# Sorted k^T copied into block order, and first FFN pieces by pairs of heads, in a block-sorted attention kernel with a squared-ReLU FFN

## The chip, the cores and the metric

The kernel runs on one core of a Trainium2 chip. The metric is the device time of one execution in microseconds; each figure is the median of several executions. The spread of the kernel before over its first three runs was 223.69 to 226.38 us. The profile is of one execution; its span (first to last instruction) is 1.5 to 2 us shorter than the device time. PE is TensorE, PEld its weight load, DVE VectorE, ACT ScalarE, POOL GpSimd, SP the engine that issues most DMAs here, and SPq its sequencer. A run counts as slow when it lies over 1.5% above the fastest of its kernel; verdicts use the fast runs alone. The clock quoted is the one granted to TensorE, 1.000 being full speed.

## The reference, cut to what matters

```python
# q, k, v: 4 batches x 8 heads x 768 x 64; sort_net: 4 x 8 x 8 x 8
P = sort_net
for _ in range(5):                      # Sinkhorn: softmax over rows, then columns
    ...
k_sorted = einsum('bhij,bhjcd->bhicd', P, k_blocks)   # blocks of 96 rows
v_sorted = einsum('bhij,bhjcd->bhicd', P, v_blocks)
scores = q_blocks @ k_sorted_blocks.T / sqrt(64)      # within a block only
attn = softmax(scores) @ v_sorted_blocks
x = attn as (3072 tokens, 512)
h = maximum(x @ w_in, 0)                # w_in 512 x 2048
out = (h * h) @ w_out                   # w_out 2048 x 512
```

The work is done in bf16 with sums in float32. The FFN is most of it: 512 up-projection matmuls of 384 columns, and 368 down-projection matmuls of 512 columns and 32 of 256.

## The kernel before

The program doesn't issue its instructions in the order of its text. Every step is handed to a planner, which simulates the engines with planned durations and thereby fixes one static list per engine. The lists are then issued as they are: an instruction that has to wait makes all that stands behind it on its engine wait too. `DUES` tells the planner after how many FFN pieces an attention step of the last batches is due, and `FIRST` gives the order of the steps of batch 0. A `Ring` is a set of buffers; an operation that takes a buffer gets the former users as dependences.

```python
DUES = {
    (0, "K"): (-15.0, -1.0, 10, 10),
    ...
    (3, "A"): (149.5, 155.0, 160.5, 162.5),
    ...
}
FIRST = ("K0 V0 K1 v1 S0 t0 S1 k2 t1 A0 V2 S2 K3 t2 A1 V3 X0 A2 S3 t3 x1 A3 X2 x3")
...
    def add(self, eng, cost, fn, deps=(), due=0, ffn=False, mode="full"):
...
            if sa is not None and (sf is None or sa < sf - 0.02
                                   or (att[0].due <= chunks and sa <= sf + 0.1)):
                pick = (sa, att)
            elif sf is not None:
                pick = (sf, ffn)
```

In the later batches the sorted keys `kn` (tokens in partitions) are turned by a transposing DMA into `kx`, in which the columns of one block lie eight elements apart. The score matmuls read them with that step as their stationary operand (the one that is loaded into the array first):

```python
        sp = plan.add("SP", 1.25, k_turn, [op, loaded(b)] + oldx)     # issue of the DMA
        k_op = plan.add("WAY", 1.6, lambda e: None, [sp])             # its way, planned
...
                            lhsT=(u.ksT[...] if not u.tiled else      # batches 0 and 1 partly
                                  kx_r[u.kx][64 * h:64 * (h + 1), NQ * hf + n::NB]),
```

An FFN unit covers 384 tokens: 16 up-projection pieces of four matmuls each (one per pair of heads, `kc`), each followed by a ReLU on ACT and a square on DVE, then the down-projections. The PSUM ring of these pieces has three banks, and a bank is free after its ReLU; the ring between ReLU and square also has three buffers:

```python
            sf, old = rf.take()
            pe = plan.add("PE", 0.65, up, xs + [landed["w_in", nt // 4]] + old, ffn=True)
            s1, old1 = rh1.take()
            r = plan.add("ACT", cost_f(HS)[0], relu, [pe] + old1)
            s = plan.add("DVE", 0.355, square, [r] + old2)
            rf.use(sf, pe, r)
```

V goes to DRAM and back for a new layout; the planner took 2 us for each way (6 us in batch 1).

## Time and profile before

| | before |
|---|---|
| time, median of 3 runs | 223.77 us |
| span of the profiled run | 222.0 us |
| mean granted TensorE clock | 1.000 |
| busy: PE, DVE, ACT | 213.3, 102.8, 120.8 us |
| stationary loads of scores, step 8 / side by side | 157 / 94 ns |
| longest wait of PE after the start | 1.06 us, for V from DRAM |

The prediction below shows the lines behind this table. One reading of that table matters more than I saw then: DVE and ACT at 46% and 54% are averages of lists that run in order. They do not say how long one instruction in such a list may last before PE feels it.

### The profile page before, as it was taken

The numbers are of one execution on the slowest core, as the hardware profiler recorded it, in microseconds if no ns is written. First come the engines' busy times: TensorE is split into PE (matmuls) and PEld (weight loads), VectorE is DVE, ScalarE is ACT, GpSimd is POOL, SyncE is SP. The second block draws the span as 40 slices with busy tenths as digits, with TensorE's granted clock in tenths as the row PEclk, the third lists the DMA queues.
The fourth block names the chain that finished last, engine by engine and source line by source line (L and its number), as shares of the span: only waits on it lengthen the run. The fifth ranks groups of instructions, "written<-read, shape, count | busy, mean of one in ns | idle before, by whom it ended". The sixth has DMA issues, their size and how long they took to land.

```text
span 222.0 us, 5101 instructions
## 1 busy us (share of the span) xinstructions
PE 213.3 (96%) x2049; PEld 120.0 (54%) x2065; DVE 102.8 (46%) x291; ACT 120.8 (54%) x249; POOL 26.5 (12%) x49
## 2 busy tenths in 40 slices
PE   8998999999999999999999999999899999999993
PEld 2576666456665555445665465445555465455562
DVE  6768477444773347602676056404655155015300
ACT  4666888217976168517864178329573276147421
POOL 7973230000000600000000240000000000000000
PEclk9999999999999999999999999999999999999999
DMA  5999999998533499189943599648982510120012
GB/s 68 201 202 207 209 206 214 209 259 229 156 82 80 90 227 223 25 218 223 206 111 83 120 176 218 128 139 177 238 175 68 118 49 3 47 94 0 3 63 78
DMA packets 46583, 31.22 MB, mean 141 GB/s; under 512 B 26016, under 2 KB 41632, under 8 KB 46560
## 3 DMA queue, kind: packets, MB, share of 16 engines
q0 software_dynamic: 12736, 13.63, 37.2%
q1 hardware_dynamic: 33824, 17.27, 30.8%
q8 instruction: 16, 0.26, 0.5%
q14 instruction: 7, 0.06, 0.1%
HBM read 29.70 MB, written 8.72 MB: 173 GB/s over the span
## 4 chain that ended last, share of the span: by engine, by line
PE 75%; DMA 17%; POOL 4%; ACT 1%; issue 1%; DVE 1%; SPq 0%; ACTq 0%
PE op L921 33%; PE hp L893 31%; DMA vb<-in_v_dram 9%; DMA w_in_bf<-in_moe_w_in_dram 5%; PE p L631 3%; PE p L814 3%; DMA vblk<-v_way 2%; PE op L955 2%; PE p L714 2%; POOL vb L300 1%; POOL kb L300 1%; DMA p_sb<-in_sort_net_dram 1%; ACT h L901 1%; DVE h L904 1%; PE qtp L511 0%
## 5 line engine op out<-in xcount | busy, mean ns | idle before, releaser
L893 PE MATMUL hp<-xT,w_in_bf 128*128 128x384 bf16 x512 | 88.9, 326 | 0.0
L921 PE MATMUL op<-w_out_bf,h 128*128 128x512 bf16 x352 | 83.3, 379 | 0.9 <-issue 0.2
L904 DVE TENSOR_TENSOR h<-h 128x384 bf16<-128x384 bf16 x128 | 44.5, 356 | 62.7 <-ACT h L901 62.3
L901 ACT ACTIVATE h<-hp 128x384 bf16<-128x384 f32 x128 | 61.6, 495 | 19.1 <-PE hp L893 15.6
L893 PEld LDWEIGHTS <-w_in_bf 128*128 128x128 bf16 x512 | 48.1, 98 | 32.1 <-issue 1.0
L921 PEld LDWEIGHTS <-h 128*128 128x128 bf16 x368 | 34.0, 98 | 37.6 <-issue 0.9
L229 ACT COPY ob<-op 128x512 f32<-128x512 f32 (+1 forms) x24 | 13.6, 567 | 62.4 <-PE op L921 59.8
L825 DVE TENSOR_TENSOR ao<-p,rec 96x512 bf16<-96x512 f32 x32 | 22.0, 687 | 1.2
L663 ACT ACTIVATE et<-p 96x384 bf16<-96x384 f32 x48 | 19.5, 489 | 3.1 <-PE p L631 3.1
L814 PEld LDWEIGHTS <-et 96*128 96x128 bf16 x256 | 11.3, 97 | 5.5 <-issue 1.7
L824 DVE RECIPROCAL rec<-p 96x8 f32<-96x8 f32 x32 | 6.4, 199 | 16.4 <-PE p L814 16.2
L1047 POOL COPY held<-xT 1x3 bf16<-1x3 bf16 (+1 forms) x2 | 0.4, 183 | 89.2 <-DMA xT<-ao 89.2
L397 PE MATMUL p<-ones 128*128 128x512 bf16 (+1 forms) x36 | 10.0, 399 | 1.1 <-DVE ones L250 1.1
L814 PE MATMUL p<-vblk,et 96*128 96x65 bf16 x192 | 8.9, 193 | 1.1 <-DMA vblk<-v_way 1.1
L231 DVE CAST vn<-p 128x768 bf16<-128x768 f32 x6 | 5.7, 958 | 8.5 <-PE p L714 8.5
L631 PEld LDWEIGHTS <-kx 64*128 64x128 bf16 x160 | 6.1, 156 | 3.9 <-issue 3.7
L631 PE MATMUL p<-qT,kx 64*128 64x96 bf16 x160 | 7.4, 228 | 0.0
L231 DVE CAST kn<-p 128x768 bf16<-128x768 f32 x5 | 4.8, 957 | 4.8 <-PE p L714 4.8
L300 POOL DMA_DIRECT2D kb<-in_k_dram x10 | 6.4, 643 | 3.5 <-DMA w_in_bf<-in_moe_w_in_dram 2.0
L300 POOL DMA_DIRECT2D qb<-in_q_dram x8 | 6.1, 770 | 4.9 <-DMA w_out_bf<-in_moe_w_out_dram 2.1
L300 POOL DMA_DIRECT2D vb<-in_v_dram x10 | 6.3, 628 | 3.3 <-DMA w_in_bf<-in_moe_w_in_dram 2.0
L654 ACT ACTIVATE et<-p 96x768 bf16<-96x768 f32 x8 | 6.2, 804 | 0.1
(80 smaller groups left out, 112.9 us busy)
## 6 DMA issues: line engine op xcount, KB each, us to landing
out_dram<-ob SPq DMA_DIRECT2D x23, 256.0 KB, 2.2
qb<-in_q_dram POOLq DMA_DIRECT2D x8, 384.0 KB, 11.0
v_way<-vn SPq DMA_DIRECT2D x6, 396.0 KB, 4.2
vblk<-v_way SPq DMA_DIRECT2D x6, 396.0 KB, 4.1
vb<-in_v_dram POOLq DMA_DIRECT2D x6, 384.0 KB, 11.4
kb<-in_k_dram POOLq DMA_DIRECT2D x6, 384.0 KB, 10.0
w_in_bf<-in_moe_w_in_dram POOLq DMA_DIRECT2D x4, 512.0 KB, 11.8
w_out_bf<-in_moe_w_out_dram POOLq DMA_DIRECT2D x4, 512.0 KB, 18.9
```

The costliest lines, as they stand in the source:

```text
L229: nc.scalar.copy(out=out, in_=in_)
L231: nc.vector.tensor_copy(out=out, in_=in_)
L300: nc.gpsimd.dma_start(out=dst, in_=src)
L397: nc.tensor.matmul(out=out, lhsT=ones, rhs=rhs, start=True, stop=True)
L631: nc.tensor.matmul(out=scp[:, h, BLK * n:BLK * (n + 1)], lhsT=(u.ksT[64 * h:64 * (h + 1), HS * hf + BLK * n:HS * hf + BLK * n + 128] if no ...
L663: nc.scalar.activation(out=et[:, h, 0:HS].rearrange("p (n c a) -> p n c a", c=C0, a=NA), in_=st["p"][0:96, h, 0:HS].rearrange("p (n a c) - ...
L814: nc.tensor.matmul(out=oup[:, h, 66 * n:66 * n + D + 1], lhsT=et_r[u.et[hf]][:, h, BLK * n:BLK * n + 128], rhs=(u.vs[:, NQ * hf + n, h, 0: ...
L825: nc.vector.tensor_tensor(out=u.ao[:, n0:n0 + NQ, :, :].rearrange("p n e d -> p e n d"), in0=ov[:, :, :, 0:D], in1=rec[:, :, :, None].to_b ...
L893: nc.tensor.matmul(out=t["hp", nt][:, 0:HS], lhsT=w_in_bf[:, kc, 128 * nt:128 * (nt + 1)], rhs=xT[:, kc, t0:t0 + HS], start=(kc == 0), sto ...
L901: nc.scalar.activation(out=t["h1", nt], in_=t["hp", nt][:, 0:HS], func=AF.Relu)
L904: nc.vector.tensor_tensor(out=t["h2"][:, nt, :], in0=t["h1", nt], in1=t["h1", nt], op=ALU.mult)
L921: nc.tensor.matmul(out=t["op", mt], lhsT=t["h2"][:, nt, 128 * mt:128 * (mt + 1)], rhs=w_out_bf[:, nt, :], start=(nt == 0), stop=(nt == NT ...
```

## The change

It has two aims. The first is to begin the FFN before the last pair of heads is ready, by cutting the first three up-projection pieces into single matmuls in the order of the pairs. The second is to speed up the scores of the later blocks by copying the turned keys on ACT or DVE, whichever the planner finds free, so that a block's 96 columns lie side by side. With them come new due times, a new order of batch 0, a planned 4 us (was 2) for V's way through DRAM, and rings cut to make room.

```diff
-FIRST = ("K0 V0 K1 v1 S0 t0 S1 k2 t1 A0 V2 S2 K3 t2 A1 V3 X0 A2 S3 t3 x1 A3 X2 x3")
+FIRST = ("V0 K0 V1 k1 t0 S0 k2 S1 t1 S2 v2 K3 A0 t2 V3 S3 t3 A1 A2 X0 X1 A3 X2 x3")
 ... (all rows of DUES are new)
-    SLACK = {"DMA": 2.5, "WAY": 1.0}
+    SLACK = {"DMA": 2.5, "WAY": 1.0, "DRAM": 0.5}
 ...
-    rkx, rkn, rqi = Ring(3), Ring(4), Ring(4)
+    rkx, rkn, rqi, rkc = Ring(2), Ring(4), Ring(3), Ring(3)
 ...
-                                  kx_r[u.kx][64 * h:64 * (h + 1), NQ * hf + n::NB]),
+                                  kc_r[u.kx][64 * h:64 * (h + 1),
+                                             HS * hf + BLK * n:HS * hf + BLK * n + 128]),
 ...
-        slow = 6.0 if b == 1 else 2.0
+        slow = 6.0 if b == 1 else 4.0
 ...
-        k_op = plan.add("WAY", 1.6, lambda e: None, [sp])
+        turned = plan.add("WAY", 1.6, lambda e: None, [sp])
 ...
+        kc, oldc = rkc.take()
+
+        def k_sort(e):
+            copy(e, kc_r[kc][:, 0:S].rearrange("p (i x) -> p x i", i=NB),
+                 kx_r[kx].rearrange("p (x i) -> p x i", i=NB))
+
+        k_op = plan.add(AD, (0.8, 0.9), k_sort, [turned] + oldc)
 ...
+            if g == 0 and nt == 0:
+                early = [rf.take() for n in range(3)]
+                for kc in range(KC):
+                    for n in range(3):
+                        last[n] = plan.add(
+                            "PE", 0.1625, lambda e, n=n, kc=kc, up=up: up(e, n, (kc,)),
+                            [x_done[0, kc, 0], landed["w_in", 0]] + early[n][1], ffn=True)
```

The loop order in `k_sort` deserves a look. With "p x i" on both sides `i` is innermost, and so the copy reads one element after the other and writes each 96 elements (192 bytes) away from the last.

> **What bounds the kernel now.** I read the page's busy table and its forty slices first, then the costliest groups, then the PE timeline of the opening, then the table of stretches, and last the waits of PE and the chain.
>
> ```profile
> PE 213.3 (96%) x2049; PEld 120.0 (54%) x2065; DVE 102.8 (46%) x291; ACT 120.8 (54%) x249; POOL 26.5 (12%) x49
> ...
> PE   8998999999999999999999999999899999999993
> ...
> PEclk9999999999999999999999999999999999999999
> ...
> L893 PE MATMUL hp<-xT,w_in_bf 128*128 128x384 bf16 x512 | 88.9, 326 | 0.0
> L921 PE MATMUL op<-w_out_bf,h 128*128 128x512 bf16 x352 | 83.3, 379 | 0.9 <-issue 0.2
> ```
>
> TensorE is in use from the first microsecond to the last stores, at full clock; no other engine is much over half. 223.77 us is the median time, 222.0 us the profiled span. From the first FFN matmul at 22.48 us to the end of the last one near 218.2 us TensorE works through one static list: up-projections in groups of four matmuls at 0.65 us, down-projections at 0.865 us, attention steps in between. So the end moves by what is taken out of that list, by how much earlier it starts, and by the holes in it. "Busy" hides two things. Dummy matmuls (line 397, there to keep the clock up) count as busy, and the 326 ns of one matmul is latency, as the next starts after about 162 ns (32 of them between 25.04 and 30.34 us). I therefore count by distances between starts.
>
> The opening, PE only:
>
> ```profile
> 18.80 0.35 PE L631 MATMUL p<-qT,kvT 64*128 64x96 bf16 x8 [0.18 <-DVE ao L825]
> 19.10 0.38 PE L679 MATMUL vbp<-ident,kvT 128*128 128x128 bf16 x4
> 20.04 0.33 PE L862 MATMUL xtp<-ident,ao 96*128 96x96 bf16 x4 [0.56 <-DVE vs L231]
> 20.21 0.42 PE L814 MATMUL p<-vs,et 96*128 96x65 bf16 x8
> 20.46 0.28 PE L397 MATMUL p<-ones 128*128 128x128 bf16 x2
> 20.82 0.33 PE L862 MATMUL xtp<-ident,ao 96*128 96x96 bf16 x4
> 20.99 0.60 PE L397 MATMUL p<-ones 128*128 128x512 bf16 x2
> 21.72 0.33 PE L862 MATMUL xtp<-ident,ao 96*128 96x96 bf16 x4
> 21.98 0.38 PE L596 MATMUL p<-w_all,kb 128*64 128x64 bf16 x12
> 22.19 0.36 PE L596 MATMUL p<-w_all,vb 128*64 128x64 bf16 x12
> ```
>
> The four "xtp" rows (the first is just ahead of this cut, at 18.03 us) turn the attention output of one pair of heads each. The FFN starts only when the last is copied out, at 22.09 + 0.36 = 22.45 us. Between them are a bare hole and two stretches of dummy matmuls. The other thing that the first piece needs is the first quarter of w_in: it was issued at 10.42 us and the shortest of the four w_in transfers took 8.9 us, so it is there at about 19.3 us; GpSimd goes on at 19.63 us after a wait for that tile, which agrees.
>
> The score matmuls (line 631), by their source line:
>
> ```profile
> L631 PEld LDWEIGHTS <-kx x160: 137/157/167, 65.8 to 167.3; 64*128 64x128 bf16 x160
> L631 PE MATMUL p<-qT,kx x160: 199/222/263, 65.8 to 167.4; 64*128 64x96 bf16 x160
> L631 PEld LDWEIGHTS <-kvT x96: 92/94/96, 14.2 to 62.2; 64*128 64x128 bf16 x96
> L631 PE MATMUL p<-qT,kvT x96: 200/203/213, 14.2 to 62.2; 64*128 64x96 bf16 x96
> ```
>
> Both kinds compute the same 64x96 products. The kx ones take their columns with a step of eight elements and load in 157 ns; the kvT ones take them side by side and load in 94 ns.
>
> The table of stretches and PE's waits show the one late hole:
>
> ```profile
> 140.00:160.00 20.00, 18.89 (x154) 9.85 (x154) 7.64 (x20) 9.88 (x21) 0.00 (x0) 1.00 0.75 170
> 160.00:180.00 20.00, 19.84 (x179) 11.23 (x180) 8.72 (x23) 10.08 (x24) 0.00 (x0) 1.00 0.53 121
> ...
> PE p L814 <- DMA vblk<-v_way: 1.1, 1, 1.1
> ```
>
> After the kernel's start this is PE's longest wait: at 157.2 us it waits 1.06 us for V on its way back from DRAM. The first column after the stretch's length is PE; the other 20 us stretches lack only 0.1 to 0.3 us each.
>
> **What the Trainium skill says.** (1) "TensorE: Matmul & The Clock Gate", section "Weight-path perf modes": the fast weight load takes 128 columns, "packed or strided", for steps up to 1,024 elements. A step of eight would so cost nothing; the trace disagrees, 157 ns against 94 ns, and the trace decides. (2) The same page, "Part 3", "The mechanism": a weight load overlaps with running matmuls only where the row group differs. The score matmuls alternate between partitions 0-63 and 64-127, and the trace agrees: 16 loads of 157 ns fit into 0.57 us. So the saving is not 16 times 63 ns; it must be read from block lengths. (3) "VectorE: DVE Perf Modes", "What auto-detection actually checks": two 16-bit elements at once need step 1 in every operand. The new copy can't have that on both sides. No row before times it.
>
> **The change part by part.**
>
> *Pieces by pairs.* The first three up-projection pieces (12 matmuls) are cut by the pair of heads that they contract over, so 9 of 12 may run before the last pair is ready. Useful room for them from 19.3 us: the hole of 0.56 us ahead of 20.04; 20.46 to 20.82, 0.36 us, around the first dummies; 20.99 to 21.72, 0.73 us. Together 1.65 us. The supply is 9 x 0.1625 = 1.46 us. No piece can use the dummy time before 19.3 us, as w_in isn't there and no load moves. The second-half sort at 21.98 us, which now hides the last copy, will instead cover the wait for PSUM after three pieces end together (each frees its bank after a ReLU of 0.495 us). The order of the early steps is rewritten too: the same 16 steps, with the last two turns still "X2 x3", and with much the same work for ACT and DVE. I take it as neutral. Expected: -1.4 us.
>
> *Copied k^T.* Starts of kx blocks of 16 to the next instruction: 103.20 to 103.83 = 0.63, 107.60 to 108.25 = 0.65, 152.76 to 153.39 = 0.63, 160.42 to 161.04 = 0.62 us. Blocks of 16 with kvT: 33.92 to 34.37 = 0.45, 56.93 to 57.37 = 0.44 us. Difference 0.19 us; there are 160/16 = 10 such blocks, all between FFN pieces on the path. Expected: -1.9 us. Three blocks (65.76, 69.83 and 111.45 us) take 0.83 to 0.90; I count no more for them, as the excess over 0.63 looks like a wait for a score buffer.
>
> What is added is ten copies of 128x768 bf16 on ACT or DVE. ACT's existing copy of that size takes 798 ns; for DVE I estimate 0.55 to 0.95 us. That is 8 us, spread over 100 us in which ACT and DVE are about half idle: off the path. They lengthen the way from transposing DMA to scores by about 1 us. In the stretch 80 to 165 us the turns are issued 4 us or more ahead of their scores in most cases. The rings of kx (3 to 2) and of paired q (4 to 3) get shorter, which may hold back a transpose but hardly a score.
>
> *Plan constants and due times.* The trip of V through DRAM is now planned as 4 us each way, where it was 2; measured medians are 4.2 and 4.1. So the scheduler puts the V product later in PE's list, behind FFN work that is ready. Expected: the 1.06 us hole goes, -1.0 us. The due times are all re-tuned; work is the same.
>
> *Sum.* -1.4 - 1.9 - 1.0 = -4.3. Against that I set 0.4 us for new small waits: a late copy before one or two scores, a ReLU held up behind a 0.8 us copy on ACT, holes opened by other due times. Net -3.9 us: 223.8 - 3.9 = **219.9 us**, a ratio of 1.018.
>
> **The rivals.**
>
> *Loads become the bound in the first 55 us.* The second V half of batch 1 lands at 42.84 us and PE waits 0.2 us for it already; loads don't move. If PE gets there 1.4 us earlier, it could simply wait longer and give back the first term: 221.3 us. Against it: that position in PE's list is computed from a planned landing time, and FFN pieces of batch 0 are left to run (12 follow the V sort at once, at 43.2 us and after). I give this one in six, and it would return part, not all.
>
> *The copy becomes a new wait.* The last batch has the least room: the transposes for k and q queue on SP from 147.3 to 161.8 us, and scores follow from 152.76. If each of its four scores came 1 us late with no FFN piece before it, that would be up to +2 us: 222 us. Against it: between these scores lie 8 to 16 FFN matmuls, and PE's list is drawn up with the copy's cost in it.
>
> *More is gained.* If the slow score blocks shrink to 0.45 as well (another 0.7 us), and the new opening order brings the last pair forward by 0.5 us, the sum is -5.5: 218.3 us.
>
> *Nothing at the opening.* If the first pieces stand in PE's list ahead of steps that attention needs, and w_in comes later than planned, they delay the last pair by as much as they gain: 221.3 us.
>
> **Range and chances.** The sure terms are the weight loads (1.6 to 2.1 us). The opening may give 0.6 to 2.0 us, the hole with the new due times between +0.8 and -1.4 us. Added up unevenly, **218.4 to 221.7 us** should hold it 8 times in 10. Over 2% faster means under 219.4 us, only 0.5 us below my figure: chance 0.35. Within 2%: 0.63. Slower by over 2%: 0.02, since the work on PE shrinks.
>
> **What would show it.** Weight loads of the tiled score matmuls at about 95 ns, and their blocks of 16 at 0.45 us. First up-projection matmuls at 19.3 to 20.2 us, few or no dummies after 19.3, and the first whole piece of the FFN done near 22.5 us. No wait of PE on "vblk" of 1 us. Ten new copies on ACT or DVE at 0.5 to 0.95 us. The last down-projection near 214.3 us instead of 218.2. I am wrong if PE shows new waits of over 1 us together for the copied k^T, for "vb", or for transposed x before a batch's first piece, or if the end of the opening doesn't move by at least 0.6 us.

## The result, and the profile after

The changed kernel took **241.56 us** (241.05 to 241.89, four runs) against 224.0 us for the kernel before in the same rounds. The ratio is 1.0757, with a 95% interval of 1.0679 to 1.0835. A ratio here and below is the mean time of one kernel's fast runs over that of the other's of the same rounds, so it is not quite the ratio of the medians quoted. (The prediction's 1.018 is the other way round, before over after.) The change made the kernel slower by some 17.6 us, where I had predicted 3.9 us of gain and had given "slower" a chance of 0.02.

The page of the changed kernel, busy times and granted clock in 40 slices (in tenths, a 9 is 90% or more):

```profile
PE 220.0 (92%) x2068; PEld 120.8 (50%) x2068; DVE 115.2 (48%) x298; ACT 135.3 (56%) x252; POOL 26.4 (11%) x49
...
PEclk9999999999979999999977999999979999999998
```

PE's share fell from 96% to 92%, and there are now dips of the clock where there were none before. The mean granted clock of this run was 0.968. DVE and ACT are still about half busy.

All instructions that write or read the new tile `kc` (count: lowest/median/highest ns):

```profile
L635 PEld LDWEIGHTS <-kc x160: 92/94/142, 68.3 to 186.2; 64*128 64x128 bf16 x160
...
L233 DVE COPY kc<-kx x6: 2072/2078/2083, 61.5 to 173.8; 128x768 bf16<-128x768 bf16 x6
...
L231 ACT COPY kc<-kx x4: 4008/4014/4071, 64.2 to 175.9; 128x768 bf16<-128x768 bf16 x4
```

The weight loads are as predicted, 94 ns. The copies are not: 2.08 us on DVE and 4.01 us on ACT, where the plan says 0.9 and 0.8 us and my estimate was 0.55 to 0.95 us.

The longest waits of PE, ACT and DVE that are new (total us, times, longest us):

```profile
DVE kc L233 <- DMA kx<-kn: 6.1, 2, 3.4
ACT h L915 <- DVE h L918: 5.4, 4, 3.5
...
PE p L635 <- DVE ao L838: 3.7, 1, 3.7
...
PE hp L907 <- ACT h L915: 3.3, 2, 2.1
...
PE p L635 <- ACT kc L231: 2.9, 1, 2.9
PE p L635 <- ACT vn L231: 2.8, 1, 2.8
```

PE's four kinds of wait add up to 3.7 + 3.3 + 2.9 + 2.8 = 12.7 us; before there was one of 1.1 us. Only the 2.9 us is a score waiting for its own copy. The others name ordinary work (the norm of the attention output, a ReLU, an eviction). The timeline shows why that work was late. This is a cut of it, all engines, from 108 to 127 us (start, duration, instruction, and in brackets the idle time before it and what ended it):

```profile
110.49 0.51 PE L635 MATMUL p<-qT,kc 64*128 64x96 bf16 x16
110.93 2.08 DVE L233 COPY kc<-kx 128x768 bf16<-128x768 bf16 x1 [2.64 <-DMA kx<-kn]
...
110.94 0.82 PE L907 MATMUL hp<-xT,w_in_bf 128*128 128x384 bf16 x4
...
112.58 1.58 DVE L918 TENSOR_TENSOR h<-h 128x384 bf16<-128x384 bf16 x4
...
113.28 0.87 ACT L915 ACTIVATE h<-hp 128x384 bf16<-128x384 f32 x2 [3.50 <-DVE h L918]
...
113.82 1.46 PE L907 MATMUL hp<-xT,w_in_bf 128*128 128x384 bf16 x8 [2.06 <-ACT h L915]
...
120.29 2.08 DVE L233 COPY kc<-kx 128x768 bf16<-128x768 bf16 x1 [3.43 <-DMA kx<-kn]
...
123.42 0.50 PE L635 MATMUL p<-qT,kc 64*128 64x96 bf16 x8 [3.74 <-DVE ao L838]
...
123.86 1.46 PE L907 MATMUL hp<-xT,w_in_bf 128*128 128x384 bf16 x4
```

Read it as a chain. DVE stands still for 2.64 us, because the next entry of its list is a copy whose transposing DMA has not landed; then it copies for 2.08 us. Four squares pile up behind it. ACT can't go on with ReLUs, as the buffers between ReLU and square are full, and stands still for 3.50 us. PE can't go on with up-projections, as the three PSUM banks are full, and stands still for 2.06 us. At 120.29 the same happens with the norm in place of the ReLU, and PE waits 3.74 us. The last line shows a second price: four up-projection matmuls took 1.46 us, while the same four took 0.82 us at 110.94; the granted clock was 0.50 from 123.4 to 125.3 us, after the wait, and 1.00 from 110.5 to 111.8. The table of stretches agrees (length, PE, PEld, ACT, DVE, POOL, granted clock, DMA share, GB/s):

```profile
120.00:140.00 20.00, 16.58 (x133) 8.31 (x133) 10.44 (x23) 5.83 (x13) 0.84 (x3) 0.83 0.30 69
...
160.00:180.00 20.00, 15.97 (x136) 9.08 (x134) 11.56 (x22) 16.40 (x22) 0.00 (x0) 0.91 0.82 165
```

In the stretch from 160 us, where the prediction shows 19.84 us of PE and 179 matmuls, it is 15.97 us and 136. Note also that the score block of 16 now ends 0.45 us after its start (110.49 to 110.94), as predicted; this gain is simply small beside the rest.

For the opening, PE of the changed kernel (the prediction shows that of the kernel before):

```profile
20.89 0.49 PE L907 MATMUL hp<-xT,w_in_bf 128*128 128x384 bf16 x2
...
22.26 0.33 PE L875 MATMUL xtp<-ident,ao 96*128 96x96 bf16 x4
```

The FFN begins 1.6 us earlier (20.89, was 22.48), but the last pair's turn comes 0.54 us later (22.26, was 21.72), and near 41 us PE waits 0.29 us for the last quarter of w_out, until 41.12 us. By then nothing of the early start is left, as the run with the pieces alone explains below: the group of 12 up-projections at 50.02 us began at 50.12 us before.

### The profile page after: what moved, and what is told of

It is laid out like the page before. It is cut to its first block, busy times and chain, and to the rows that moved or that the text cites. A ratio compares the mean times of both kernels' runs of the same rounds, so it can differ in the third digit from the quotient of the medians.

```text
span 240.1 us, 5116 instructions
## 1 busy us (share of the span) xinstructions
PE 220.0 (92%) x2068; PEld 120.8 (50%) x2068; DVE 115.2 (48%) x298; ACT 135.3 (56%) x252; POOL 26.4 (11%) x49
## 4 chain that ended last, share of the span: by engine, by line
PE 60%; DMA 18%; DVE 7%; ACT 5%; issue 4%; POOL 4%; SPq 1%; ACTq 0%; POOLq 0%; DVEq 0%
PE op L947 31%; PE hp L907 21%; DMA w_out_bf<-in_moe_w_out_dram 9%; DMA kx<-kn 5%; DMA w_in_bf<-in_moe_w_in_dram 4%; DVE kc L233 3%; PE p L827 3%; DVE h L918 2%; ACT kc L231 2%; PE p L635 2%; ACT h L915 2%; PE p L719 2%; PE op L981 1%; DVE ao L838 1%; POOL vb L304 1%
## 5 line engine op out<-in xcount | busy, mean ns | idle before, releaser
L907 PE MATMUL hp<-xT,w_in_bf 128*128 128x384 bf16 x512 | 91.2, 331 | 3.4 <-ACT h L915 3.3
L947 PE MATMUL op<-w_out_bf,h 128*128 128x512 bf16 x368 | 88.2, 387 | 0.3 <-DMA w_out_bf<-in_moe_w_out_dram 0.3
L915 ACT ACTIVATE h<-hp 128x384 bf16<-128x384 f32 x128 | 62.9, 504 | 25.8 <-PE hp L907 15.5
L231 ACT COPY kc<-kx 128x768 bf16<-128x768 bf16 x4 | 16.1, 4027 | 0.0
L635 PE MATMUL p<-qT,kc 64*128 64x96 bf16 x160 | 6.6, 218 | 9.9 <-DVE ao L838 3.7
L233 DVE COPY kc<-kx 128x768 bf16<-128x768 bf16 x6 | 12.5, 2078 | 6.1 <-DMA kx<-kn 6.1
L827 PEld LDWEIGHTS <-et 96*128 96x128 bf16 x256 | 12.4, 103 | 5.7 <-issue 2.1
L635 PEld LDWEIGHTS <-kc 64*128 64x128 bf16 x160 | 4.6, 101 | 14.7 <-issue 10.9
L401 PE MATMUL p<-ones 128*128 128x128 bf16 (+1 forms) x39 | 9.8, 377 | 1.3 <-DVE ones L252 1.1
L827 PE MATMUL p<-vblk,et 96*128 96x65 bf16 x192 | 10.6, 204 | 0.2 <-ACT et L668 0.2
## 6 DMA issues: line engine op xcount, KB each, us to landing
w_out_bf<-in_moe_w_out_dram POOLq DMA_DIRECT2D x4, 512.0 KB, 19.3
```

Of the source, the lines that this page charges most:

```text
L231: nc.scalar.copy(out=out, in_=in_)
L233: nc.vector.tensor_copy(out=out, in_=in_)
L401: nc.tensor.matmul(out=out, lhsT=ones, rhs=rhs, start=True, stop=True)
L635: nc.tensor.matmul(out=scp[:, h, BLK * n:BLK * (n + 1)], lhsT=(u.ksT[64 * h:64 * (h + 1), HS * hf + BLK * n:HS * hf + BLK * n + 128] if no ...
L827: nc.tensor.matmul(out=oup[:, h, 66 * n:66 * n + D + 1], lhsT=et_r[u.et[hf]][:, h, BLK * n:BLK * n + 128], rhs=(u.vs[:, NQ * hf + n, h, 0: ...
L907: nc.tensor.matmul(out=t["hp", nt][:, 0:HS], lhsT=w_in_bf[:, kc, 128 * nt:128 * (nt + 1)], rhs=xT[:, kc, t0:t0 + HS], start=(kc == 0), sto ...
```

## The experiments

18 kernels ran, and all gave the reference's result within tolerance. Times are medians, always beside runs of the kernel before on the same chip. Two forms of the theory of the slow copy are called A1 and A2 in the quoted texts: A1 says that the step of 96 elements on the side that is *written* costs, A2 that the step of eight on the side that would be *read* costs as much. The rivals to a slow copy were that the new lists and due times are bad by themselves, that the copy's place in an in-order list hurts whatever it costs (by its wait for the DMA), and that the opening or the V trip gives the time away.

### First set: the parts

**Loop order of the copy swapped**, nothing else; the planned lists are the same.

```diff
-            copy(e, kc_r[kc][:, 0:S].rearrange("p (i x) -> p x i", i=NB),
-                 kx_r[kx].rearrange("p (x i) -> p x i", i=NB))
+            copy(e, kc_r[kc][:, 0:S].rearrange("p (i x) -> p i x", i=NB),
+                 kx_r[kx].rearrange("p (x i) -> p i x", i=NB))
```

> The changed kernel with one edit: the k^T copy runs over the same 768 elements in the other loop order, so that it writes side by side and reads with a step of eight (before: reads side by side, writes with a step of 96). The instruction lists of all engines are otherwise the same, in the same order. Theory A (the copy's write order makes it 2.08 us on DVE and 4.03 us on ACT, and that holds up the ReLUs behind it, then PE): copies at 0.5 to 0.9 us, no wait of PE over 1 us at the scores, time 218.5 to 221.5 us. Rival B (the early pieces and new due times leave PE without ready work): copies shorter, but time still over 230 us. Rival C (a strided copy costs the same whichever side has the step): copies stay at 2 and 4 us, time 241 us.

232.14 us, ratio 1.0373 (1.0336 to 1.0409). The copies of this kernel, by tile:

```profile
L233 DVE COPY kc<-kx x6: 834/854/862, 61.3 to 168.0; 128x768 bf16<-128x768 bf16 x6
...
L231 ACT COPY kc<-kx x4: 1562/1576/1579, 63.5 to 169.6; 128x768 bf16<-128x768 bf16 x4
```

Both copy the same bytes from and to the same places; only the order differs. This order costs 0.85 instead of 2.08 us on DVE, 1.58 instead of 4.01 us on ACT. That is worth 241.56 - 232.14 = 9.4 us of the kernel's time, shown by one edit that changes nothing else (the traces show one and the same order of instructions on PE, ACT and DVE). But 8.0 us over the kernel before remain, where theory A had forecast 218.5 to 221.5 us, and PE still has a wait of 4.0 us at the scores. So theory A explains a part.

**The change without the copy**: scores read `kx` with the step of eight again, everything else of the change stays, and the planner draws the lists anew.

```diff
-        k_op = plan.add(AD, (0.8, 0.9), k_sort, [turned] + oldc)
+        k_op = turned
```

> The changed kernel without the copy: scores read k^T with a step of eight as in the kernel before; early pieces, early order, planned DRAM trips and due times stay as changed. Theory A: the loss is gone, 221 to 223.5 us (only the 1.9 us of cheaper weight loads is missing from what the rest gives). Rival B: over 230 us.

227.18 us, ratio 1.0163 (1.0109 to 1.0218). Neither forecast holds: most of the loss hangs on the copy, but some 3 us do not. In this kernel PE waits for V from DRAM for 3.4 us (two waits). Probably the due times fit a plan with the copy in it, and without it V's product comes too early; that is not shown.

**The kernel before with the slow copy alone.**

```diff
+        k_op = plan.add(AD, (0.8, 0.9), k_sort, [turned] + oldc)   # and kc, its ring, scores from kc
```

> The kernel before with the copy alone, in the write order of the change; due times, early order and pieces as before. Theory A: slow by itself, 233 to 243 us, PE waits of several us at scores and ReLUs from 62 us on, none before. Rival B: within 2 us of 224 us, since neither due times nor pieces are there.

239.90 us, ratio 1.0697 (1.0657 to 1.0737): the copy alone, in the old due times, brings nearly the whole loss.

**The kernel before with the pieces by pairs alone.**

```diff
+            if g == 0 and nt == 0:
+                early = [rf.take() for n in range(3)]  # as in the change
```

> The kernel before with only the first three up-projection pieces cut by pairs; early order and due times as before. My prediction's first term says -1.4 us: 222.4 us. What the two traces show speaks for less: in the changed kernel the last pair was ready some 0.5 us later than before, as pieces stand ahead of attention steps in PE's list; then -0.2 to -0.6 us, 223.2 to 223.6 us. Theories A and B both allow it; over 226 us would speak for B.

224.73 us, ratio 1.006 (1.001 to 1.011). No gain, and a miss of both forecasts. Its trace shows where the lead goes (PE only):

```profile
24.42 1.15 PE L895 MATMUL hp<-xT,w_in_bf 128*128 128x384 bf16 x6
26.04 4.06 PE L895 MATMUL hp<-xT,w_in_bf 128*128 128x384 bf16 x24 [0.46 <-ACT h L903]
```

Only five of the nine matmuls run before the last pair's turn at 21.44 us (one at 20.19, four from 20.71 us), and the hole of 0.56 us ahead of the second turn stays. Then PE waits 0.46 us for a ReLU: the PSUM banks are full, and in ACT's list two attention steps of 0.80 and 0.81 us (at 24.10 and 24.80 us) stand ahead of the ReLUs that would free them. The first down-projection starts at 37.31 us. In the eleven profiles with the old opening, the old due times and no early pieces it starts between 37.34 and 37.73 us, so no lead is left. In eight of these eleven PE then waits 0.2 to 0.7 us for the last quarter of w_out, as it does here (0.60 us); a lead that lasted would have met that wait too.

### Second set: the copy by itself

**What the copy costs in each form**: 21 copies of 128x768 bf16 at the end of the kernel before, in seven forms on each of three engines (its time is that of the added work and means nothing).

```diff
+    forms = {"plain": ..., "write96": ..., "read8": ..., "write8": ..., "read96": ..., "write2": ..., "read2": ...}
+    for name, (fo, fi) in forms.items():
+        for eng, dst in zip(("ACT", "DVE", "POOL"), flat): ...
```

> The kernel before with 21 copies of 128x768 bf16 after its last work: seven address patterns (plain; inner write step 96; inner read step 8; inner write step 8; inner read step 96; inner write step 2; inner read step 2) on ACT, DVE and GpSimd in turn. It measures the copy by itself. Theory A1 (a step on the writing side costs, growing with the step): write 96 at 2.08 us on DVE and 4.03 on ACT, write 8 near that on DVE or between, reads with a step at 0.85 us or less on DVE. Rival A2 (only the step's size in bytes matters, on either side): read 96 as slow as write 96, read 8 as write 8.

All forms by engine (lowest/median/highest ns):

```profile
L1106 POOL COPY kn<-kn x7: 825/1495/4025, 151.8 to 164.8; 128x768 bf16<-128x768 bf16 x7
...
L231 DVE COPY kn<-kn x7: 353/820/2082, 213.4 to 220.3; 128x768 bf16<-128x768 bf16 x7
...
L229 ACT COPY kn<-kn x7: 831/1476/4017, 223.4 to 236.0; 128x768 bf16<-128x768 bf16 x7
```

One by one, in ns, read from the timeline of the same run:

| inner step of the form | DVE | ACT | GpSimd |
|---|---|---|---|
| 1 on both sides | 353 | 834 | 825 |
| written with step 96 | 2082 | 4017 | 4025 |
| written with step 8 | 1889 | 3582 | 3630 |
| written with step 2 | 606 | 1045 | 1078 |
| read with step 96 | 820 | 1476 | 1495 |
| read with step 8 | 866 | 1536 | 1556 |
| read with step 2 | 561 | 831 | 1053 |

A1 is supported and A2 is not: a step of eight costs 1889 ns on the written side and 866 ns on the read side. The step's length matters little beyond eight; the side matters, at steps of 8 and 96, by a factor of 2.2 to 2.7. A rearranging copy has to have a step on one side, and this side can be chosen by the order of the loops alone. What in the engines or the memory makes it so is not shown.

**The kernel before with the well-ordered copy alone** (planned as in the change, 0.8 and 0.9 us).

```diff
+            copy(e, kc_r[kc][:, 0:S].rearrange("p (i x) -> p i x", i=NB),
+                 kx_r[kx].rearrange("p (x i) -> p i x", i=NB))
```

> The kernel before with the copy alone, writing side by side (0.85 us on DVE, 1.57 us on ACT). If the copy's length is all that counts, the weight loads win: 222 to 224.5 us. If the copies also block DVE and ACT while they wait for their transposing DMA (theory D), the loss stays: 226 to 231 us, with waits of DVE or ACT for the transposed k^T of several us in all, and PE behind them.

228.22 us, ratio 1.0189 (1.0156 to 1.0222). Even a good copy, added to the old due times, costs 4.3 us by medians where the faster scores were to save 1.9. The time and the waits of DVE and ACT for transposed k^T (3.7 us in all) are what theory D had forecast; length and waiting are told apart in the third and fourth sets.

**The same on GpSimd**, which is 12% busy and has no FFN work in its list; planned as 1.6 us, measured 1.62 us.

```diff
-        k_op = plan.add(AD, (0.8, 0.9), k_sort, [turned] + oldc)
+        k_op = plan.add("POOL", 1.6, k_sort, [turned] + oldc)      # gpsimd.tensor_copy
```

> The kernel before with the copy alone, writing side by side, on GpSimd, which has nothing else to do there; so no ReLU or square can stand behind a copy that waits for its DMA. Theory D: the waits of PE are gone and the cheaper weight loads show, 221.5 to 223 us. If the later k^T itself is what costs: PE waits at the scores remain, 225 us or more.

225.13 us, ratio 1.004 (0.9985 to 1.0095). On an engine where nothing stands behind the copy, twice the duration costs almost nothing. But there is no gain either: theory D had forecast 221.5 to 223 us. No wait of PE is put down to `kc`; the largest after the opening are for DVE's norm (1.6 us in three), q's load (1.3 us) and V from DRAM (0.9 us in two).

**The change, well ordered, with the transposing DMA planned at 5.0 us** instead of 1.6, so that the copy would stand later in the lists.

```diff
-        turned = plan.add("WAY", 1.6, lambda e: None, [sp])
+        turned = plan.add("WAY", 5.0, lambda e: None, [sp])
```

> The changed kernel, writing side by side, with the transposing DMA planned at 5.0 us where it was 1.6: the copies go later into the lists of ACT and DVE and so wait less there. Theory D: the waits of DVE and ACT for transposed k^T shrink from 13.6 us to under 4, time 225 to 229 us (232.1 with the early places; 227.2 without any copy). Rival: the copies' length alone does it, then 231 us or more.

243.83 us, ratio 1.0912 (1.0838 to 1.0987): a plain miss. Waits for `kx` were gone, as intended, but a new wait took their place: PE stood for the turned attention output for 6.2 us in four waits, and the planner gave ACT 8 of the 10 copies. Attention as a whole came so late that the FFN ran out of input. A due time has two sides.

### Third set: place, length or lists

**A copy of 8 columns in the copy's place** in the kernel before, scores reading `kx` as before. It takes 0.16 to 0.20 us but stands in the list and waits for the DMA exactly as the full copy does.

```diff
-            copy(e, kc_r[kc][:, 0:S]..., kx_r[kx]...)
+            copy(e, kc_r[kc][:, 0:8], kx_r[kx][:, 0:8])
```

> The kernel before with, in the place of each k^T copy in the lists of ACT and DVE, a copy of only 8 columns of the same transposed k^T (so it waits for the same transposing DMA but takes under 0.25 us); the scores wait for it and read k^T with a step of eight as before. It takes the copy's length away and leaves its wait in the queues. Theory D (blocking while waiting for the DMA is the cost of the well-ordered copy): 227 to 230 us, near the 228.2 of the full copy. Rival (the copy's length of 0.85 and 1.57 us is the cost): 223.5 to 225 us.

226.62 us, ratio 1.0098 (1.0042 to 1.0153): between the two forecasts. The fourth set shows how much of it is the list.

**The whole change, well-ordered copy on GpSimd.**

```diff
-        k_op = plan.add(AD, (0.8, 0.9), k_sort, [turned] + oldc)
+        k_op = plan.add("POOL", 1.6, k_sort, [turned] + oldc)
```

> The whole change, but the copy writes side by side and runs on GpSimd. If the copy's two faults (write order, standing ahead of ReLUs and squares) are all that is wrong with it, this is the version without the copy (227.2 us) less the 1.5 to 1.9 us of cheaper weight loads: 225 to 226 us, and PE waits at the scores under 1 us each. If k^T comes too late through GpSimd (1.6 us each): 227 us or more.

229.97 us, ratio 1.0255 (1.0206 to 1.0303). A miss by 4 us, though PE waits only 0.4 us for `kc` itself: taking the copy out of the in-order lists of ACT and DVE does not bring the change to par. In the due times of the change, PE waits for V from DRAM 4.1 us in two waits here.

**Only the planned DRAM trip** (4 us) in the kernel before.

```diff
-        slow = 6.0 if b == 1 else 2.0
+        slow = 6.0 if b == 1 else 4.0        # and the class "DRAM" with its slack
```

> The kernel before with only the planned time of V's trip through DRAM changed, 4 us each way. My prediction's third term: the 1.06 us wait for V goes, 222.7 to 223.3 us. Rival: the due times, not the planned trip, set where the V product stands in PE's list; then the wait stays and the time is 223.5 to 224.5 us.

224.84 us, ratio 1.0025 (0.9944 to 1.0106). The hole at V did not close. PE in its trace:

```profile
159.88 0.66 PE L814 MATMUL p<-vblk,et 96*128 96x65 bf16 x16 [2.11 <-DMA vblk<-v_way]
```

The product with V does stand two pieces later in PE's list, behind 24 up-projection matmuls where there were 16. But the longer planned trip moved the read of V as well: it was issued at 154.34 us (before 152.72) and landed at 159.84 (before 157.19).

**Only the due times of the change** in the kernel before; the opening order `FIRST` stays the old one.

```diff
-DUES = {...}
+DUES = {...}   # the change's
```

> The kernel before with only the due times of the change. If they are what makes the version without the copy slow (227.2 against 224.0, two waits for V of 1.7 us each): 226 to 228 us, with those waits. If the new early order and the pieces cost it: within 1 us of 224.

226.73 us, ratio 1.0104 (1.001 to 1.0198). In this set four of the seven runs of the kernel before fell in the slow state (clock 0.969 to 0.991); the ratios use the three fast ones, 223.47 to 224.78 us, and their intervals are wide. Two of the four runs of this kernel had a clock of 0.99; the other two, at full clock, took 225.45 and 225.75 us, about 1 us over the fast runs of the kernel before. The two waits for V from DRAM that the text expected are not there; PE waits 2.2 us for the load of V of batch 1 and 0.9 us for turned q instead.

### Fourth set: the lists without the copy

The planner makes a new list for every edit, so "the change without the copy" above differs from the change in more than the copy. These two keep the lists of all other instructions exactly, by planning the copy and issuing nothing for it:

```diff
         def k_sort(e):
-            copy(e, kc_r[kc][:, 0:S]..., kx_r[kx]...)
+            pass                    # the DMA writes into the ring of kc; scores read it with step 8
```

**The list of the kernel before with the well-ordered copy, no copy issued:**

> The kernel before's due times, TensorE's list exactly as in the run with the well-ordered copy alone, but no copy is issued; scores read k^T with a step of eight. If the list drawn up around the copy costs nothing by itself: 223.5 to 224.5 us, and the copies cost 4.3 plus the 1.9 us that their cheaper weight loads gave. If the list costs (scores in halves, more alternation): 225.5 to 226.5 us, and the 8-column copy's 226.6 was mostly list.

225.63 us, ratio 1.0072 (1.0019 to 1.0124), in the band of "the list costs". The traces show that this run, the 8-column copy and the well-ordered copy alone have one and the same order of instructions on PE, ACT and DVE (the copy apart). So the list costs 0.7%, the wait brings it to 1.0%, and the full copy, its faster scores included, to 1.9%; the first two intervals overlap.

**The list of the change, no copy issued:**

> The changed kernel, TensorE's list exactly as it is, but no copy is issued; scores read with a step of eight. It should agree with the earlier version without copy, whose list differs a little: 226.5 to 228 us. Then 241.6 less this is what the copies cost as they are, 232.1 less this what well-ordered ones cost.

227.38 us, ratio 1.0108 (1.0063 to 1.0153); its three fast runs have a median of 227.03. So the change's lists cost about 2.7 us before any copy runs, as expected. PE waits 2.7 us for V in two waits here. The change itself has no such wait, probably because everything else is later.

**The kernel before with the well-ordered copy planned at what it takes** (1.6 us on ACT, 0.87 us on DVE; the planner then puts nine of ten on DVE).

```diff
-        k_op = plan.add(AD, (0.8, 0.9), k_sort, [turned] + oldc)
+        k_op = plan.add(AD, (1.6, 0.87), k_sort, [turned] + oldc)
```

> The kernel before with the well-ordered copy, planned at the lengths measured (1.6 us on ACT, 0.87 on DVE; before 0.8 and 0.9). The scheduler should then give most of the ten to DVE. If the planned cost matters: 225 to 227 us against 228.2. If not, 227.5 to 228.5 us.

225.95 us, ratio 1.0087 (1.0037 to 1.0138). Telling the planner the truth halves the loss of the well-ordered copy (1.0189 before). It does not make the copy pay.

**One due time of the kernel before, nothing of the change.**

```diff
-    (3, "A"): (149.5, 155.0, 160.5, 162.5),
+    (3, "A"): (152.5, 155.0, 160.5, 162.5),
```

> The kernel before with one due time changed: the first product with V of the last batch three FFN pieces later (152.5 for 149.5), without any part of the change. If the 1.06 us wait for V is simply a step that stands too early in the list: the wait goes and 222.8 to 223.3 us, faster than before by 0.3 to 0.5%. If the delay comes back later, at the last batch's turned x: 223.7 to 224.3 us, with a new wait there.

**222.96 us** (222.64 to 223.36, six runs), ratio 0.993 (0.9901 to 0.9959). It beats both kernels. The stretch from 140 us in its trace, where the prediction shows 18.89 us of PE for the kernel before:

```profile
140.00:160.00 20.00, 20.00 (x162) 10.56 (x161) 7.98 (x22) 10.53 (x22) 0.00 (x0) 1.00 0.73 160
```

This was as forecast. The hole at V is gone, and the gain of 1.4 us by medians is of its size.

### Fifth set: mended versions

**The change, well ordered and honestly planned.**

```diff
-  k_op = plan.add(AD, (0.8, 0.9), k_sort, ...)   # written with step 96
+  k_op = plan.add(AD, (1.6, 0.87), k_sort, ...)  # read with step 8
```

> The whole change with the copy mended: writes side by side, planned at 1.6 us on ACT and 0.87 us on DVE. By the same step that took the copy alone from 1.019 to 1.009 of before, the changed kernel should come from 232.1 us to 226 to 230 us; it can't be better than its lists without any copy by more than the 1.9 us of the weight loads: 225.5 us at best. Over 231 us would say that planned length does not matter here.

233.50 us, ratio 1.041 (1.0324 to 1.0496): a miss, no better than the swapped loop order alone; by the text's own sign the planned length does not matter here. All ten copies are on DVE, at a median of 0.854 us, and yet PE waits up to 3.4 us. A cut of its timeline from 104 to 122 us, all engines:

```profile
108.88 1.21 SPq L771 DMA_TRANSPOSE kx<-kn  x1
...
115.94 0.83 DVE L233 COPY kc<-kx 128x768 bf16<-128x768 bf16 x1 [4.98 <-DMA kx<-kn]
...
117.93 0.35 PE L635 MATMUL p<-qT,kc 64*128 64x96 bf16 x8 [3.37 <-DVE ao L838]
```

The copy is short now, but DVE stands still for 4.98 us in front of it. In the due times of the change, two reads of V, of 396 KB each, are issued on the same queue just ahead of the transposing DMA (from 107.78 us), and in this profile the slowest such DMA took 6.9 us from issue to landing (6.5 us in the change, 4.7 us in its list without copies), where the longest was 4.3 us in the kernel before. The plan counts on 1.6 us and a slack. In all, DVE waits 11.0 us for these DMAs. That V's transfers are what slows the transpose is the likely reading; no run moved them alone. The amount of waiting does not decide, though. In the run with the old due times and the same planned lengths (1.0087), a transpose took 6.5 us too, and DVE waits 10.3 us in all, once even longer:

```profile
92.31 8.81 PE L931 MATMUL op<-w_out_bf,h 128*128 128x512 bf16 x40
...
99.38 0.85 DVE L231 COPY kc<-kx 128x768 bf16<-128x768 bf16 x1 [5.65 <-DMA kx<-kn]
```

That wait fell into a stretch of 40 down-projections, and PE did not stop. The 4.98 us fell among up-projections and attention products, and PE stopped for 3.37 us. The two traces suggest that what PE is doing meanwhile decides; no run tested it.

**The kernel before, mended copy and one later due time together** ((3, "A") at 153.5).

```diff
+        k_op = plan.add(AD, (1.6, 0.87), k_sort, [turned] + oldc)
-    (3, "A"): (149.5, 155.0, 160.5, 162.5),
+    (3, "A"): (153.5, 155.0, 160.5, 162.5),
```

> The kernel before with the mended copy and the first product with V of the last batch four FFN pieces later. If the 1.9 us wait for V in the run with the mended copy alone was all that stood against it: 223.5 to 224.5 us. If this beats 222.96 us (the due time alone), the copy pays; I give that one in ten.

225.46 us, ratio 1.0086 (1.0017 to 1.0155): again a miss. The wait for V is gone, but a wait of 1.8 us of an attention product for DVE's norm takes its place. (Its profile is that of the slowest run, 227.28 us at a clock of 0.992; the other three took 225.35 to 225.54 us.)

## Why the prediction was wrong, point by point

**The step that failed is the copy: "That is 8 us, spread over 100 us in which ACT and DVE are about half idle: off the path."** It failed twice.

First, the size. I took 0.55 to 0.95 us for DVE and 798 ns for ACT from a copy "of that size". The ACT copy I used (`qT<-qtp`, from PSUM) writes in order. I had noted that the new one can't have a step of 1 on both sides, but drew the consequence only for DVE's faster modes and for no more than a factor of about two. The copy took 2.08 and 4.01 us: 6 x 2.08 + 4 x 4.01 = 28.5 us in place of 8. The loop order alone is 9.4 us of the kernel's time (shown by the swap).

Second, "off the path". A well-ordered copy of 0.85 and 1.58 us still leaves the changed kernel 8.0 us behind. Half-idle engines with in-order lists are not off the path when PE has three banks in hand: three pieces at 0.65 us are about 2 us (an estimate from the planned length), and a DMA that is 2.6 to 5 us late, with a copy standing in front of ReLU, square or norm, can take more than that. My rival of "up to +2 us" had the copy delay only its own scores. In the trace, only 2.9 of PE's 12.7 us are that (enough for my own sign of being wrong, over 1 us of waits for the copied k^T); the rest hit work that has nothing to do with the copied keys.

By medians the loss of 17.6 us divides so: the list of the change without any copy 2.7 us; the well-ordered copy in that list, less what the faster scores give, another 8.0 - 2.7 = 5.3 us; the order of writing 9.6 us (17.6 - 8.0; 9.4 without correcting for the two sets' runs of the kernel before). Within the 5.3 us, waiting and length are not separated. In the *old* due times they are, and there waiting alone costs little (226.62 against 225.63 us for the same list without a copy, intervals that overlap) and length more (228.22 us). Slow transposes do not set the change apart: with the old due times one took 6.5 us as well, in both runs with the well-ordered copy alone.

**Weight loads, -1.9: right in kind and size.** 157 became 94 ns, and blocks of 16 shrank from 0.63 to 0.45 us. It never showed as time gained, because each version of the copy tried cost at least as much as it brought: on ACT and DVE about 1.009 at best, on GpSimd 1.004.

**Opening, -1.4: wrong.** The pieces did run early (20.19 us alone, 20.89 us in the changed kernel, where I named 19.3 to 20.2), but the pieces alone give 1.006. The first step that failed is the room: five matmuls ran ahead of the last turn, not nine. The second is the sort that was to "cover the wait for PSUM": it doesn't, and PE waits 0.46 us for a ReLU behind ACT's attention steps. The rival "loads become the bound in the first 55 us" holds in part and with the wrong load: not V of batch 1, but the last quarter of w_out near 41 us, for which PE mostly waited before the change too. I had not looked up when it lands. The rival that the pieces delay the last pair is not borne out by the run with the pieces alone: its last pair is copied out at 22.16 us. In all seven kernels with the new order of the early steps that copy ends at 22.99 to 23.22 us, in all thirteen with the old order at 22.16 to 22.55. So it is that order, alone or together with the rest, that delays the pair, and I had taken it as neutral; it had no run of its own.

**The hole at V, -1.0: right that it can be had, wrong about what gives it.** The planned trip alone leaves it (1.0025, a wait of 2.1 us), since it puts off the read of V along with the product. One due time later by three pieces takes it away, without the rest of the change.

**Small waits, 0.4: mis-sized.** The change's list without copies costs 2.7 us (1.0108). The due times alone gave 1.0104, but about 1 us in the runs at full clock.

**The chance of 0.02 for "slower"** rested on "the work on PE shrinks". That was the wrong question. In the two profiles the span grew by 18.1 us: PE's idle time by 11.4 us (20.1, was 8.7), and its busy time by 6.7 us (220.0, was 213.3) with nearly the same matmuls. The lower clock accounts for about that much (an estimate: 220.0 us x 0.032 = 7.0 us).

**What I read from the Trainium skill.** In (1) the page doesn't say that a step costs nothing; I concluded it. In (2) the trace shows that loads of alternating row groups overlap with matmuls, not that only these do: in the same trace a full-row load of w_in (22.65 to 22.75 us) lies within two full-row matmuls (22.48 to 22.82 and 22.65 to 22.98 us, by the profile's modelled ends). In (3) the section names a second mode with two elements at once, for one source in SBUF, that asks for no step of 1; the slow copy, at 2.71 ns per column, shows no sign of either.

## What to carry to other kernels

When a copy must rearrange, put the step on the side that is read and write in order; here the same copy took 0.85 or 2.08 us by that choice alone. Before placing new work on a half-idle engine with an in-order list, ask what stands behind it, how late its input can be, how many buffers the bounding engine has left meanwhile, and what kind of work it will be doing; plan with measured durations, and measure a new instruction's form before you plan with it. Look for a single wait that a due time can remove before restructuring: one number gave 0.7% here, and the restructured versions gave none.

## What the Trainium skill lacked or had wrong

- "Vector Engine (DVE) Microarchitecture Reference", section "5.2 Measured stream behaviour on trn2", bears on the copy, and I had missed it when I predicted: for 32-bit words it lists 2.50 to 2.51 ns per column when the destination alone steps by 24 words, against 1.054 ns in order. The runs lie near it for a bf16 destination with a step of 96 elements: 2082 ns for 768 columns is 2.71 ns per column. For reads it lists 1.73 ns when one of two sources hops at every element, and notes that a one-source op ran at the full rate all the same. The copy has one source, and with a read step of 96 it took 820 ns, 1.07 ns per column: it agrees with the note, and paid no such price.
- "VectorE: DVE Perf Modes", "What auto-detection actually checks", speaks only of which mode is lost by a step. I took the plain mode for the worst case; it is not: 866 ns (read with step 8) but 1889 ns (written with step 8). A pointer to section 5.2 above would have helped.
- No page that I found gives a price for strided writes on ACT or GpSimd: 834 to 4017 ns and 825 to 4025 ns for the same 128x768 bf16 copy. "SBUF — State Buffer", "Specifications (TRN2)", row "Cachelines", says that every crossing into a new 16-byte line pays, without a figure and without telling reads from writes; on ACT the runs show 3582 ns against 1536 ns for a step of 16 bytes.
- "TensorE: Matmul & The Clock Gate", "Weight-path perf modes", calls the fast weight load's pattern "packed or strided" and gives no cost of the step: 157 ns with a step of eight bf16, 94 ns side by side.
- "Perfetto Trace Analysis", "Identifying the Most-Contended Engine", takes occupancy for Vector and Scalar as a fair measure of how close they are to roofline. Here DVE and ACT at 48% and 56% held PE up for 12.7 us. The page does say, under "Optimizing Scalar/DVE Operations", that engines which aren't saturated can cause bubbles on others, and advises to break up instructions. It lacks the other case that the runs show: a short instruction (0.83 us) that waits 4.98 us for its DMA, with PE stopped for 3.37 us soon after.
